# A fused attention and feed-forward kernel: first batch with tokens on partitions, its opening in the planner, new positions

## The chip, the cores and the metric

The kernel runs on one core of one Trainium2 chip. The metric is the device time of one execution in microseconds. A core has five engines with queues of their own: TensorE (PE, matrix products; its weight loads are PEld), VectorE (DVE), ScalarE (ACT), GpSimd (POOL) and SyncE (SP). PE writes into eight PSUM banks of 128 x 512 float32; all other data on the chip lies in SBUF.

## The reference

For each of 8 batches and 8 heads, with 1024 tokens of 64 values, the keys and values are first projected along the tokens to 64 rows, then plain softmax attention runs against those rows, and its output (8192 tokens of 512 values) goes through a gated feed-forward layer.

```python
k_proj = np.einsum('ks,bhsd->bhkd', E, k)
v_proj = np.einsum('ks,bhsd->bhkd', F, v)
scores = scale * np.matmul(q, k_proj.transpose(0, 1, 3, 2))
scores = scores - np.max(scores, axis=-1, keepdims=True)
attn = np.exp(scores)
attn = attn / (np.sum(attn, axis=-1, keepdims=True) + 1e-09)
attn_out = np.matmul(attn, v_proj)          # then (B, H, S, D) -> (B * S, H * D)
gate = 1.0 / (1.0 + np.exp(-(x @ w_gate)))  # x: 8192 x 512, w_gate, w_val: 512 x 1536
out = gate * (x @ w_val) @ w_out            # w_out: 1536 x 512
```

## The kernel before

**Units of work.** Tokens are handled in 16 blocks of 512, two to a batch. A block needs its part of the attention output, transposed (tiles `xT`), then the gate and value products (`wG`, `wV`), the gating into `hT`, and the output product with `wO`. Matmul operands are bfloat16. Blocks 1 to 15 compute gate and value with seven products in place of eight on halved matrices (`seven`, line 1253, called by `quad_jobs`, 1292): sums of the weights (`w_sum`, 1198, into `tG`, `tV`) and of `xT` (`x_sums`, 1193, into `xS`) are made once, and partial results are added by ScalarE and VectorE. Three such steps K make a block, so block b has K = 3b to 3b + 2, and K counts to 48. The output product does the same (`o_jobs`, 1435; sums `o_sum` of `wO` into `wT`, `s_sum` of `hT`), except in block 0 and in the last block, where it is plain (`o_plain`, 1411). Block 0's gate and value products are plain too (`plain_steps`, 1135): 96 matmuls of 512 columns.

**The attention of batches 1 to 7.** `kv` projects k and v of a batch in one bank (1560); ScalarE keeps the result in `kpd` and `vpD`, and SP transposes `kpd` to `kpD` and q to `qT` by DMA (`turn_kd`, `transpose_q`). A score tile holds 128 tokens on the partitions and 4 heads times 2 groups of 64 rows (`score`, 1699). VectorE takes the maxima of its eight groups (`highest`); they are subtracted either by TensorE with a matmul of 512 columns against `minus`, or by VectorE (`lower`, 1731; the choice is `s0` to `s7`, one for each of a batch's eight tiles). ScalarE takes the exponential into `pt`, SP transposes by DMA to `eT`, and `outs` multiplies with `vpD`, whose extra column of ones gives the sums. VectorE takes their reciprocal and divides by them, or ScalarE copies the bank out and GpSimd divides (`d0` to `d2`, one for each of three groups of heads), into `xt`, which SP transposes into `xT`. `pt` and `xt` lie in the buffer `KVs` that the loads of k and v fill. In batch 1, k and v are projected one after the other (`apart_jobs`), and q and `kpd` are transposed by TensorE (`turn_q_pe`, `turn_kd_pe`).

**The first batch.** It has another form: scores lie with the projected rows on the partitions, the exponential is taken without a maximum, the sums come from a matmul with a pattern (`h_den`), a reciprocal of 128 columns (`h_rec`) and a second matmul that spreads them (`h_bc`), and VectorE multiplies the output with them (`h_scale`). The first 512 tokens (block 0) run in an order written out by hand (lines 1010 to 1063), with matmuls on `ident` as fillers (`busy`); the second 512 (block 1) are jobs (`second_half`, 1078).

**What sets the order.** From 21.8 us on, every piece of work is a job with an engine, a position, a release time and a cost by a model (`Scheduler`, 148). The planner steps through modelled time and gives each free engine the ready job of lowest position, as long as its position is within `window` of the first unplaced PE job, and PSUM banks and buffers can be had. The outcome is a fixed order for each queue. Positions come from the table `AT`. POOL first issues all loads of `start_loads` (624) in order: these DMAs convert float32 to bfloat16.

Of the kernel before, what the change touches and what calls it, by code (L numbers as in the profile page):

```python
# [7 lines left out]
ALU = mybir.AluOpType  # L8
# [16 lines left out]
    window=2.535, step=0.142, lag=0.29, ostep=0.443, tanh=1.746, hidden=-1.635, oa=0.798, ob=3.658,  # L25
    sums=1.354, late=0.034, sc=1.515, scs=0.326, out=4.0, outs=0.181, loads=1.714, gap=0.063,
    kv=5.561, tq=3.75, xa=6.242, xb=6.53, w0=3.112, ws=0.6, kv1=2.867, vv1=3.987, wo=3.716, f_wo=0,
    qt1=2.06, sc1=4.73, scs1=0.041, late1=0.543, out1=4.796, outs1=0.123, osum=4.574, loads2=7.657,
    tq2=5.48, kv2=7.388, xa2=5.884, xb2=1.618, o0=4.191, o0s=0.26, xs1=4.106, sc2=1.232, end=4.616,
    pesub=0.843, s0=1, s1=1, s2=1, s3=0, s4=0, s5=0, s6=0, s7=0, o0p=1, o1p=0, o2p=0, o3p=1, x1=0,  # L30
    x2=0, x3=0, x4=0, g1=0, g2=0, g3=0, g4=1, d0=1, d1=0, d2=0, dsub=-0.833, dexp=0.747, dinv=0.205,
    ddiv=1.082, dplus=0.007, dsnap=-1.085, dmerge=-0.547, dcopy=0.897, dturn=-0.257, pdma=0.454,
    pact=0.007, pdve=0, ppool=0.112, lag0=0.208, lag1=-0.622, lag2=0.103, lag3=0.091, lag4=0.09,
    lag5=0.002,
# [113 lines left out]
class Scheduler:  # L148
# [4 lines left out]
    def __init__(self, banks, bufs, t0, window, landed):  # L153
        self.jobs, self.now, self.t0, self.window, self.landed = [], None, t0, window, landed
        self.writers, self.readers = {}, {}
        self.free = {
            "bank": {b: t0 for b in banks},
            "buf": {b: t0 for b in bufs},
        }
        self.clean = {b: False for b in banks}  # L160
        self.groups = []
        self.reads = []
        self.more = {"ACT": AT["pact"], "DVE": AT["pdve"], "POOL": AT["ppool"]}

    def job(self, eng, pos, body, release=0.0, name=""):
        j = Job(eng, pos, body, release, name)
        self.jobs.append(j)
        self.now = j
        body()
        self.now = None  # L170
        return j
# [72 lines left out]
    def take(self, j, t):  # L244
        got = []
        for s in j.slots:
# [4 lines left out]
            if s.kind == "bank":  # L251
                if s.clean:
                    mine = [b for b in mine if self.clean[b]]
                elif s.dirty:
                    rough = sum(not c for c in self.clean.values()) + sum(self.clean[b] for _, b in got)
                    mine = [b for b in mine if not self.clean[b] or rough < 3]
# [54 lines left out]
    def run(self):  # L311
        engines = ("PE", "ACT", "DVE", "POOL", "SP")
        self.busy = {e: self.t0 for e in engines}
# [15 lines left out]
        while left:  # L329
            moved = True  # L330
            while moved:
# [4 lines left out]
                for e in engines:  # L336
# [9 lines left out]
                    if best is not None:  # L346
                        self.open[e].remove(best)
                        self.place(best[3], t)
                        left -= 1
                        moved = True  # L350
# [9 lines left out]
def bass_linformer_attn__then__ffn_glu_sigmoid_kernel(  # L360
# [20 lines left out]
    with contextlib.ExitStack() as es:  # L381
# [28 lines left out]
        pats = within([P, 4, 32], FP32)  # L410
        identf = within([P, P], FP32)
        bsel8f = within([P, 4, 2, 64], FP32)
        early[0], used[0] = wT[:, :, :, :].rearrange("p a b c -> p (a b c)"), 0
        bsel8 = within([P, 4, 2, 64], BF16)
        kp = within([P, NR, DH], BF16)
        rhi = within([P, 256], BF16)
        rhl = within([P, 256], BF16)
        kpD0 = within([P, H, DH], BF16)
        vpD0 = within([P, H, DH], BF16)
        rden = within([P, 256], FP32)  # L420
        quad = sbuf("quad", [P, 1], FP32)
        row_f = sbuf("row_f", [P, 1], FP32)
        rows = sbuf("rows", [P, 4, 32], FP32)
        half = sbuf("half", [P, 2], FP32)
        ident = sbuf("ident", [P, P], BF16)
        dsel8 = sbuf("dsel8", [P, 2, 4, 32], BF16)
# [23 lines left out]
        xu = ost  # L450
# [10 lines left out]
        F0, F1, F2, F3, A0, A1, A2, A3 = range(8)  # L461

        plan = Plan()
        sched = Scheduler(range(8), range(2 + NB), 21.8, AT["window"], 38.8)
# [6 lines left out]

        class Ring:
            def __init__(self, banks):
                self.banks, self.turn = banks, 0

            def next(self):
                b = self.banks[self.turn % len(self.banks)]
                self.turn += 1
                return b

        whole = Ring(
            (A0, A1, A2, A3, F0)
            + (A0, A1, F1, F2, A2)
            + (A3, F0, A0, A1, F1)
            + (A3, F0, A2)
            + (F2, A0, A1, F1)
            + (A3, A2, A0, A1, A3, A0)
        )
# [67 lines left out]
        def total(eng, o, a, b, op, r, w, n):  # L556
            fn = lambda e: e.tensor_tensor(o, a, b, op)  # L557
            if eng == "POOL":
                pool(fn, r, w, cost=n / 410 + 0.06, port=True)
# [8 lines left out]
        def load(o, i, w, sem, r=(), nbytes=0):  # L568
            add("POOL", lambda e: e.dma_start(o, i), r=r, w=w, dma=sem, cost=0.88, nbytes=nbytes)  # L569
# [14 lines left out]
        def load_kv_heads(n, src, R):  # L584
            hh = slice(4 * R, 4 * R + 4)
            load(
                KV[n][:, hh, :],
                src[0].rearrange("h (p t) d -> p h (t d)", t=NT)[:, hh, :],
                [("KV", n, R)],
                f"KV{n}{R}",  # L590
            )
# [32 lines left out]
        def start_loads():  # L624
# [24 lines left out]
            load_w(3)  # L649
            load_w(4)  # L650
            load_w(5)

        def constants():
# [10 lines left out]
            dve(lambda e: e.tensor_copy(pats[:, 0, :], count[:, 0:32]), ["count"], ["pats"])  # L664
            for i, n in ((1, 8), (2, 4)):
                dve(
                    lambda e, i=i, n=n: e.tensor_copy(
                        pats[:, i, :].rearrange("p (a b) -> p a b", b=n),
                        count[:, 0:n].unsqueeze(1).to_broadcast([P, 32 // n, n]),
                    ),  # L670
                    ["count"],
                    ["pats"],
                )
            dve(
                lambda e: e.tensor_scalar(
                    pats[:, 3, :].rearrange("p (a b) -> p a b", b=16),
                    count[:, 0:16].unsqueeze(1).to_broadcast([P, 2, 16]),
                    8.0,
                    -1.0,
                    op0=ALU.is_ge,  # L680
                    op1=ALU.mult,
                ),
                ["count"],
                ["pats"],
            )
            dve(
                lambda e: e.transpose(
                    rows[:, :, :].rearrange("p a b -> p (a b)"),
                    pats[:, :, :].rearrange("p a b -> p (a b)"),
                ),  # L690
                ["pats"],
                ["rows"],
            )
            dve(
                lambda e: e.tensor_tensor(row_f[:, :], rows[:, 0, 0:1], quad[:, :], ALU.add),
# [11 lines left out]
            if any(AT[f"s{n}"] > 0 for n in range(8)):  # L707
                dve(
                    lambda e: e.tensor_scalar(
                        minus[:, :], count[:, :], row_f[:, 0:1], -1.0, op0=ALU.is_equal, op1=ALU.mult  # L710
                    ),
                    ["count", "row_f"],
                    ["minus"],
                )
            for n, op in ((0, ALU.is_ge), (1, ALU.is_lt)):
                dve(
                    lambda e, n=n, op=op: e.tensor_scalar(
                        half[:, n : n + 1], row_f[:, :], 64.0, None, op0=op
                    ),
                    ["row_f"],  # L720
                    [("half", n)],
                )
            for t, k, m, w in ((dsel8, "dsel8", 8, 4),):
                for n in range(2):
                    for i in range(w):
                        dve(
                            lambda e, t=t, m=m, n=n, i=i: e.tensor_scalar(
                                t[:, n, i, :].rearrange("p (a b) -> p a b", b=m),
                                count[:, 0:m].unsqueeze(1).to_broadcast([P, 32 // m, m]),
                                half[:, n : n + 1],  # L730
                                2.0 * i,
                                op0=ALU.subtract,
                                op1=ALU.is_equal,
                            ),
                            ["count", ("half", n)],
                            [(k, n)],
                        )
            for t, k, m, i, v in (
                (bsel8f, "bsel8f", 8, 1, 0.25),
                (bsel8, "bsel8", 8, 1, 0.5),  # L740
            ):
                dve(
                    lambda e, t=t, m=m, i=i, v=v: e.tensor_scalar(
                        t[:, :, :, :].rearrange("p c h d -> p (c h) d"),
                        count[:, 0:m].unsqueeze(2).to_broadcast([P, m, 64]),
                        rows[:, i, 0:1],
                        v,
# [1235 lines left out]
```

## Time and profile before

| | us |
|---|---|
| median of three runs (lowest, highest) | 529.25 (528.47, 529.41) |
| the profiled execution | 528.34 |
| its span, first to last instruction | 526.5 |
| busy: PE, DVE, ACT, POOL | 512.5, 434.3, 372.2, 127.3 |

The granted TensorE clock was 0.999 in the mean. A line of a group gives the kernel's line, engine, operation, tiles and shapes, the count, then the busy time and the mean length of one instruction in ns, then the idle time of the engine just before them and what ended it. Matmuls and VectorE instructions overlap their neighbours, so the mean length is more than the distance from start to start. Line 528 is the helper of all matmuls, 542 of all ScalarE instructions and 569 of all loads. Times in the text are us from the span's start.

### The profile page before, as it was taken

Reading aid. Unit: us, or ns where it says so; the run is one execution under the profiler, and the core shown is the slowest. Engines: PE = TensorE matmul, PEld = TensorE weight load, DVE = VectorE, ACT = ScalarE, POOL = GpSimd, SP = SyncE. Lnnn points to the kernel's source line nnn. Section 1 sums busy time; section 2 is a strip of 40 time slices with the busy share of each in tenths; the row PEclk is TensorE's granted clock in tenths of the full one; section 3 lists DMA queues with packets and bytes.
Section 4 is the critical chain, followed back from the end, with each engine's and each line's share of the span. In section 5 each row is a group of like instructions: output and inputs, shape, how many; then the busy total and the mean of one; then the engine's idle time right before and its main releaser. Section 6 shows DMA issues by size and latency. Waiting matters only on the chain.

```text
span 526.5 us, 12200 instructions
## 1 busy us (share of the span) xinstructions
PE 512.5 (97%) x4823; PEld 427.1 (81%) x4826; DVE 434.3 (82%) x862; ACT 372.2 (71%) x689; POOL 127.3 (24%) x146
## 2 busy tenths in 40 slices
PE   4999989999999999999999999999999999999997
PEld 4545847878988898888988899878988889888883
DVE  6579798879997899779996899968997799978570
ACT  2556965867786878768878687768777688766661
POOL 9710002602232044020530214220440205011200
PEclk9999999999999999999999999999999999999999
DMA  9999738995699657974689565994369956210103
GB/s 159 199 198 205 123 73 168 160 182 121 101 168 212 95 134 131 230 137 114 104 130 225 99 152 82 189 193 94 107 121 231 152 105 107 71 41 21 62 30 131
DMA packets 134569, 70.53 MB, mean 134 GB/s; under 512 B 92912, under 2 KB 126192, under 8 KB 134512
## 3 DMA queue, kind: packets, MB, share of 16 engines
q0 software_dynamic: 34320, 29.89, 36.6%
q1 hardware_dynamic: 100192, 39.86, 36.6%
q8 instruction: 38, 0.62, 0.5%
q14 instruction: 19, 0.16, 0.1%
HBM read 60.29 MB, written 16.78 MB: 146 GB/s over the span
## 4 chain that ended last, share of the span: by engine, by line
PE 86%; DMA 9%; POOL 1%; ACT 1%; DVE 1%; issue 1%; POOLq 0%; SPq 0%; ACTq 0%
PE pA L528 45%; PE pF L528 41%; DMA KVs<-in_v_dram 8%; DMA xT<-KVs 1%; POOL KVs L569 1%; ACT spare L542 1%; ACT KVs L542 0%; POOL Qb L569 0%; DVE spare L1247 0%; DVE wT L917 0%; DVE KVs L1807 0%; DVE hT L1316 0%; DVE wT L823 0%; ACT ost L542 0%; ACT vpD L542 0%
## 5 line engine op out<-in xcount | busy, mean ns | idle before, releaser
L542 ACT ACTIVATE spare<-pF 128x512 f32<-128x512 f32 (+1 forms) x165 | 95.2, 589 | 41.7 <-PE pF L528 39.6
L557 POOL TENSOR_TENSOR hT<-hT,hS 128x512 bf16<-128x512 bf16 x42 | 52.4, 1272 | 263.0 <-PE pA L528 122.2
L542 ACT ACTIVATE spare<-pA 128x512 f32<-128x512 f32 (+1 forms) x117 | 67.9, 586 | 32.0 <-PE pA L528 30.5
L528 PE MATMUL pA<-wO,hT 128*128 128x256 bf16 (+1 forms) x370 | 54.4, 286 | 1.0 <-ACT spare L542 1.0
L542 ACT ACTIVATE spare<-spare 128x512 f32<-128x512 f32 x71 | 44.5, 628 | 11.4 <-DVE spare L1247 11.2
L1247 DVE TENSOR_TENSOR spare<-pF,spare 128x512 f32<-128x512 f32 x57 | 39.1, 687 | 12.4 <-ACT spare L542 11.1
L1316 DVE SCALAR_TENSOR_TENSOR hT<-spare,pF 128x512 bf16<-128x512 f32 x59 | 40.1, 682 | 11.1 <-PE pF L528 7.4
L1247 DVE TENSOR_TENSOR spare<-pA,spare 128x512 f32<-128x512 f32 x53 | 36.0, 686 | 13.0 <-ACT spare L542 5.9
L528 PEld LDWEIGHTS pA<-wO,hT 128*128 128x128 bf16 x372 | 36.1, 98 | 9.8 <-DVE topf L1720 1.0
L1316 DVE SCALAR_TENSOR_TENSOR hT<-spare,pA 128x512 bf16<-128x512 f32 x54 | 36.7, 682 | 6.0 <-PE pA L528 5.6
L528 PE MATMUL pF<-xT,wG 128*128 128x256 bf16 (+1 forms) x244 | 39.3, 283 | 0.4 <-ACT pF L542 0.4
L528 PE MATMUL pF<-xS,tG 128*128 128x256 bf16 x256 | 38.4, 273 | 0.0
L528 PE MATMUL pF<-wO,hT 128*128 128x256 bf16 (+1 forms) x227 | 35.3, 295 | 0.1
L528 PE MATMUL pA<-wT,hT 128*128 128x256 bf16 x264 | 35.0, 273 | 0.2 <-ACT spare L542 0.2
L528 PE MATMUL pA<-xT,wV 128*128 128x256 bf16 (+1 forms) x208 | 33.9, 285 | 0.0
L528 PE MATMUL pF<-xT,wV 128*128 128x256 bf16 (+1 forms) x200 | 32.8, 286 | 0.0
L528 PE MATMUL pA<-wT,hS 128*128 128x256 bf16 x240 | 31.4, 272 | 0.0
L528 PE MATMUL pF<-xS,wV 128*128 128x256 bf16 x208 | 31.2, 273 | 0.0
L528 PEld LDWEIGHTS pF<-xT,wG 128*128 128x128 bf16 x244 | 23.6, 98 | 6.4 <-ACT pF L542 0.7
L528 PE MATMUL pA<-xS,wG 128*128 128x256 bf16 x192 | 28.6, 273 | 0.0
L528 PEld LDWEIGHTS pA<-wT,hT 128*128 128x128 bf16 x264 | 25.4, 98 | 3.2 <-ACT spare L542 0.5
L528 PEld LDWEIGHTS pF<-wO,hT 128*128 128x128 bf16 x228 | 22.1, 98 | 7.2
(193 smaller groups left out, 1252.2 us busy)
## 6 DMA issues: line engine op xcount, KB each, us to landing
out_dram<-ost SPq DMA_DIRECT2D x64, 256.0 KB, 2.8
KVs<-in_k_dram POOLq DMA_DIRECT2D x16, 512.0 KB, 7.7
KVs<-in_v_dram POOLq DMA_DIRECT2D x16, 512.0 KB, 13.4
Qb<-in_q_dram POOLq DMA_DIRECT2D x14, 512.0 KB, 17.9
wO<-in_moe_w_out_dram POOLq DMA_DIRECT2D x1, 1536.0 KB, 12.8
wG<-in_moe_w_gate_dram POOLq DMA_DIRECT2D x5, 256.0 KB, 19.2
wV<-in_moe_w_val_dram POOLq DMA_DIRECT2D x5, 256.0 KB, 19.9
Qb<-in_q_dram POOLq DMA_DIRECT2D x4, 256.0 KB, 14.7
```

What stands on the lines that cost most here:

```text
L528: lambda e: e.matmul(o, lhsT, rhs, **kw),
L542: lambda e: e.activation(o, i, func, scale=scale),
L557: fn = lambda e: e.tensor_tensor(o, a, b, op)
L569: add("POOL", lambda e: e.dma_start(o, i), r=r, w=w, dma=sem, cost=0.88, nbytes=nbytes)
L1247: lambda e: e.tensor_tensor(PB(b)[:, :] if stay else BF(s), PB(b)[:, :], BF(s), ALU.add),
L1316: lambda e: e.scalar_tensor_tensor(o, y.rearrange("p (j c) -> p j c", j=2), 1.0, x.rearrange("p (j c) -> p j c", j=2), ALU.add, ALU.mult,),
```

## The change

- The first batch takes the form of the others: tokens on partitions, maximum and subtraction, exponential into a buffer. The sum (`total0`) and its reciprocal follow on VectorE, and the weights are multiplied with it before the product with v (`norm0`, on GpSimd for heads 0 to 3 of the first 512 tokens, else on VectorE). TensorE transposes them (`turn_p0`), and four products in quarters of the array give the output already transposed (`h_xo`), which is copied into `xT`. `h_den`, `h_rec`, `h_bc`, `h_scale` and their patterns go.
- All of it is jobs of the planner, which starts at 8.3 us in place of 21.8; fillers are put where PE has nothing before 21.0 modelled us.
- Loads of the first k, and of half the first v, are halved (25 issues in place of 22); weights come in the order 0, 3, 1, 4, 2, 5; block 0's products follow that order.
- The memsets of `kpd` and `vpD` move from GpSimd to VectorE and to the start.
- Batch 1 projects k and v together and turns q and k by DMA. The load of `wO` no longer waits for v.
- `s0` to `s2` become 0, `d2` becomes 1; four weight sums go to GpSimd; keys of dependences are finer (a half of the heads each).
- Costs in the model change, all positions are new, `window` goes from 2.535 to 39.691.
- The last quarter of the last block is computed, copied and stored in two halves of 256 columns.

```diff
 AT = dict(
-    window=2.535, step=0.142, lag=0.29, ostep=0.443, tanh=1.746, hidden=-1.635, oa=0.798, ob=3.658,
+    window=39.691, step=0.195, lag=0.031, ostep=0.461, tanh=24.746, hidden=-7.261, oa=0.642, ob=4.537,
...
-    pesub=0.843, s0=1, s1=1, s2=1, s3=0, s4=0, s5=0, s6=0, s7=0, o0p=1, o1p=0, o2p=0, o3p=1, x1=0,
-    x2=0, x3=0, x4=0, g1=0, g2=0, g3=0, g4=1, d0=1, d1=0, d2=0, dsub=-0.833, dexp=0.747, dinv=0.205,
+    xa2=2.02, xb2=5.69, o0=8.301, o0s=1.088, xs1=-1.514, sc2=-4.038, end=3.656, pesub=8.049, s0=0, s1=0, s2=0,
+    s3=0, s4=0, s5=0, s6=0, s7=0, o0p=1, o1p=0, o2p=0, o3p=1, x1=0, x2=0, x3=0, x4=0, g1=0, g2=0, g3=0, g4=1,
+    d0=1, d1=0, d2=1, dsub=-4.028, dexp=-11.886, dinv=-7.839, ddiv=-2.87, dplus=-7.33, dsnap=7.354,
...
+FB = dict(
...
+    f_pv00=1, f_pv01=0, f_pv10=0, f_pv11=0, f_s00=0, f_s01=1, f_s10=0, f_s11=1, f_n00=1, f_n01=0, f_n10=0,
...
+    f_dk=1, f_w2=1, f_late=0, f_q1=0, f_q2=0, f_wsG0=0, f_wsG1=1, f_wsG2=0, f_wsV0=0, f_wsV1=0, f_wsV2=0,
...
-        sched = Scheduler(range(8), range(2 + NB), 21.8, AT["window"], 38.8)
+        busy0 = {"PE": 8.3, "ACT": 8.4, "DVE": 7.0, "POOL": 18.3, "SP": 8.3}
+        sched = Scheduler(range(8), range(2 + NB), 8.3, AT["window"], 38.0, busy0, 21.0)
...
             for R in range(2):
-                load_kv_heads(0, k, R)
-            for R in range(2):
+                for th in range(2):
+                    load_part(0, k, R, th)
                 load_q_half(0, 0, R)
-            for R in range(2):
-                load_kv_heads(1, v, R)
+            load_part(1, v, 0)
+            for th in range(2):
+                load_part(1, v, 1, th)
             load_w(0, 0)
             load_w(0, 1)
+            load_w(3)
             load_w(1)
-            load_w(2)
             for R in range(2):
                 load_q_half(0, 1, R)
-            load_w(3)
             load_w(4)
+            load_w(2)
             load_w(5)
...
+        def total0(t, R, s):
+            i = inv[:, 16 * t + 8 * R : 16 * t + 8 * R + 8]
+            x = BF(s).rearrange("p (n k) -> p n k", n=8)
+            ks = [("inv", t, 4 * R + h) for h in range(4)]
+            dve(lambda e: e.tensor_reduce(i, x, mybir.AxisListType.X, ALU.add), [bf_(s)], ks)
+            dve(lambda e: e.reciprocal(i, i), ks, ks, n=30)
+
+        def norm0(t, R, s, eng):
+            i = inv[:, 16 * t + 8 * R : 16 * t + 8 * R + 8].unsqueeze(2).to_broadcast([P, 8, 64])
+            x = BF(s).rearrange("p (n k) -> p n k", n=8)
+            o = pt0[:, t % 2, 512 * R : 512 * R + 512].rearrange("p (n k) -> p n k", n=8)
+            fn = lambda e: e.tensor_tensor(o, x, i, ALU.mult)
...
+            def tile(hf, R, t):
+                new_group()
+                bk = new_bank()
+                sb = None if hf and FB["f_late"] else new_buf()
+                p = FB[f"sc{hf}{R}"] + 0.003 * (t % 2)
+                job("PE", p, lambda: score(t, R, bk), name="sc")
+                job("DVE", p, lambda: highest(0, t, R, bk), name="top")
+                job("PE" if by_pe(0, t, R) else "DVE", p, lambda: lower(0, t, R, bk), name="sub")
...
+                job("ACT", p, lambda: exp0(bk, sb), name="exp")
+                job("DVE", p + FB["dsum"], lambda: total0(t, R, sb), name="psum")
+                eng = "POOL" if FB[f"f_n{hf}{R}"] > 0 else "DVE"
+                job(eng, p + FB["dnorm"], lambda: norm0(t, R, sb, eng), name="norm")
...
-                r=[("pt", 3, 1)] if AT["f_wo"] else [("KV", 1, R) for R in range(2)],
+                r=[] if FB["f_w2"] else [("pt", 3, 1)] if AT["f_wo"] else [("KV", 1, R) for R in range(2)],
...
-        for K in range(3, 6):
-            quad_jobs(K, K)
-        apart_jobs(1, 0, AT["kv1"])
-        apart_jobs(1, 1, AT["vv1"])
-        turn_q_pe(AT["qt1"])
+        for K in range(1, 6):
+            if K > 2 or FB[f"f_q{K}"]:
+                quad_jobs(K, K)
+        if FB["f_dk"]:
+            kv_jobs(1, AT["kv1"])
...
+        if FB["f_dq"]:
+            turn_q(AT["qt1"])
...
             h = hT[blk % 2]
-            for tt in range(4):
+            last = blk == 2 * B - 1
+            for tt in range(3 if last else 4):
...
+            for x in range(2 * last):
+                new_group()
+                b = new_bank()
+                cc = slice(256 * x, 256 * x + 256)
```

More of the change, by code (lines that the diff above doesn't have):

```diff
@@ L312, in run @@
         engines = ("PE", "ACT", "DVE", "POOL", "SP")
-        self.busy = {e: self.t0 for e in engines}
+        self.busy = dict(self.busy0)
         self.pipe, self.held, self.lock = self.landed, 0.0, 0.0
@@ L706, in constants @@
                 )
[L707 to L722, printed above, removed]
@@ L757, in project_consts @@
             for g in range(2):
-                b = whole.next()
+                b = g
                 for t in range(4):
@@ L847, in VPD @@
-        def VPD(R):
-            return [("vpD0", h, g, R) for h in range(2) for g in range(2)]
+                mm(7, bank[7][:, 0:P], ident[:, :], ident[:, :], ["ident"], n=P)
         def h_qt(hf, R, rr, bk):
@@ new lines, in keep_v0, with turns @@
+        def keep_v0(R, bk, g, eng):
+            gg, hh = slice(64 * g, 64 * g + 64), slice(4 * R, 4 * R + 4)
+            i = PB(bk)[gg, 0:256].rearrange("p (h d) -> p h d", h=4)
+            copy(eng, vpD[0][gg, hh, g, 0:DH], i, [], [("vpD", 0, g, R)], bk, 270 if eng == "ACT" else 380)
+        def turns(b, src, keys, n=4):
+            ob = PB(b)[:, :].bitcast(BF16)
+            for x in range(n):
+                mm(b, ob[:, x * P : (x + 1) * P], src(x), ident[:, :], keys + ["ident"], tr=True, n=P)
@@ new lines, in total0 @@
+        def total0(t, R, s):
[9 more added lines that the diff above has]
+            fn = lambda e: e.tensor_tensor(o, x, i, ALU.mult)
+            r, w = [("inv", t, 4 * R + h) for h in range(4)] + [bf_(s)], [("pt0", t % 2, R)]
+            if eng == "POOL":
+                pool(fn, r, w, cost=1.11, port=True)
+            else:
+                dve(fn, r, w)
@@ L1135, in plain_steps @@
         def plain_steps():
-            for m in range(NF):
+            for m in [m for q_ in range(3) for m in (2 * q_, 2 * q_ + 1, 2 * q_ + 6, 2 * q_ + 7) if not (q_ and FB[f"f_q{q_}"])]:
                 new_group()
@@ L1582, in keep_kd @@
                 [],
-                [("kpd", g)],
+                [("kpd", g, x) for x in range(2)],
                 b=bk,
@@ L1685, in turn_kd_pe @@
                     ident[:, :],
-                    [("kpd", 0), ("kpd", 1), "ident"],
+                    [("kpd", g, x) for g in range(2) for x in range(2)] + ["ident"],
                     tr=True,
@@ L1792, in invert @@
                 [],
-                [("inv", t, hh[0])],
+                [("inv", t, h) for h in range(*hh)],
                 b=bk,
```

815 lines of the change are left out of this document (357 added, 458 removed).

## The prediction

> **What bounds the kernel now.** I read the page's busy table, then the waits of TensorE, then busy time by stretches, then the groups of the engines.
>
> ```profile
> span 526.5 us, 12200 instructions
> ...
> PE 512.5 (97%) x4823; PEld 427.1 (81%) x4826; DVE 434.3 (82%) x862; ACT 372.2 (71%) x689; POOL 127.3 (24%) x146
> ```
>
> TensorE is busy for 97% of the span. Its waits (engine, line, released by: sum, times, longest):
>
> ```profile
> PE pA L528 <- DMA EF<-in_F_dram: 5.7, 1, 5.7
> PE pA L528 <- ACT spare L542: 1.9, 3, 1.0
> ```
>
> The first is the start; the second, with two short ones, is 2.3 us of stall between 64 and 73 us. The same by stretches (busy us and instructions of PE, PEld, DVE, ACT, POOL, then granted clock, DMA share, GB/s):
>
> ```profile
> 0.00:20.00 20.00, 12.71 (x181) 9.93 (x181) 11.83 (x36) 7.16 (x15) 19.21 (x33) 1.00 1.08 174
> 20.00:24.00 4.00, 3.58 (x54) 2.15 (x47) 2.62 (x7) 2.65 (x6) 3.40 (x5) 1.00 1.45 195
> 24.00:34.00 10.00, 10.00 (x60) 4.85 (x58) 5.75 (x16) 4.28 (x8) 0.74 (x1) 1.00 1.45 197
> 34.00:50.00 16.00, 16.00 (x143) 7.54 (x142) 15.94 (x39) 9.83 (x20) 0.98 (x2) 1.00 1.29 204
> 50.00:60.00 10.00, 9.99 (x112) 8.45 (x112) 6.35 (x12) 9.32 (x18) 0.78 (x1) 1.00 1.21 198
> 60.00:80.00 20.00, 17.71 (x150) 11.85 (x148) 18.91 (x33) 14.30 (x27) 0.69 (x1) 1.00 0.32 67
> 80.00:510.00 430.00, 429.21 (x4071) 375.30 (x4071) 369.02 (x719) 321.04 (x594) 101.51 (x106) 1.00 0.70 129
> ```
>
> From 80 to 510 us TensorE misses 0.8 us: there every microsecond of matmul counts, and VectorE has room (369 of 430). From 34 to 50 and from 60 to 80 VectorE is full: there its work may count too. So the sum is TensorE's work taken away, against later starts and new stalls.
>
> **Rates.** Busy time of pipelined groups overlaps, so I take distances between starts. The last plain blocks start 12 matmuls of 512 columns every 2.59 us: 0.216 each. Eight 128-column transposes of q last 0.62 with 0.22 for the last one: 0.057 each. VectorE's full-width operations start every 0.60 us, whatever they are:
>
> ```profile
> 72.75 0.69 DVE L1747 TENSOR_TENSOR pF<-pF,topf 128x512 f32<-128x512 f32 x1
> 73.35 0.68 DVE L1720 TENSOR_REDUCE topf<-pA 128x8 f32<-128x512 f32 x1
> 73.95 0.68 DVE L1720 TENSOR_REDUCE topf<-pF 128x8 f32<-128x512 f32 x1
> ```
>
> **1. Subtractions leave TensorE (s0 to s2 become 0).** The groups that go, and those of step 2:
>
> ```profile
> L528 PE MATMUL pF<-top,minus 128*128 128x512 bf16 x13 | 4.8, 379 | 0.0
> L528 PE MATMUL pA<-ident,Qb 128*128 128x128 bf16 x44 | 3.5, 220 | 0.4 <-DMA Qb<-in_q_dram 0.4
> L528 PE MATMUL pA<-top,minus 128*128 128x512 bf16 x8 | 3.0, 379 | 0.0
> L528 PE MATMUL pA<-ident,kpd 128*128 128x128 bf16 x8 | 0.6, 219 | 0.0
> ```
>
> 13 + 8 = 21 matmuls of 0.216: **-4.5 us**, three in each of batches 1 to 7. VectorE takes 21 x 0.60 = 12.6 us more and gives back 28 divisions of 256 columns (d2 becomes 1). A 128x256 division shows 406 ns, about 0.33 between starts: 9.3 us. Net +0.5 us in a batch of 61 us, of which 369/430, or 86%, were busy: covered. ScalarE copies 28 times 260 columns for it (a 256-column copy shows 384 ns; +10 us in all, on 71%), GpSimd divides them (822 ns for 384 columns, so 0.55: +15 us, on 24%). If the cover fails in a batch, TensorE waits; that is rival 2.
>
> **2. Batch 1 turns q and k by DMA.** 32 + 8 transposes x 0.057 = **-2.3 us** of TensorE; VectorE loses 2 evictions and ScalarE 3. The joint projection of k and v is worth under 0.1 (12.2 us in 6 batches against 2.1 for each of batch 1's two parts, busy). In their place come 5 DMA transposes on SP; such an issue takes 1.24 us there and lands after 3.2 to 3.6. Batch 1's scores so come some 4 us later than after a transpose on TensorE, and block 0's stores stand behind these issues on SP. Batch 1 is wanted when block 2 begins, near 81 us, and until then TensorE has blocks 0 and 1: covered unless the loads are late.
>
> **3. First batch, second half of the tokens.** It removes 16 transposes, 16 score, 16 output and 32 sum and broadcast matmuls, 3.5 to 4 us by their rates; it brings 16 + 16 transposes, 16 score matmuls of 128 columns (48 x 0.057 = 2.7), 2 subtractions (0.4) and 16 output matmuls (0.9): 4.0. **0** on TensorE, +-0.5. On VectorE: four maxima 2.4, two subtractions 1.2, four sums with reciprocals 2.8, four products 2.4, about 7 copies or parts 2.6, so 11.4 against 5.6 before (reciprocal 0.95, scalings 3.2, splitting and copies 1.4): +5.8 us between 30 and 50 us, where it was full. Four weight sums move to GpSimd (-1.5), batch 1 has 3 subtractions more and 4 divisions fewer (+0.5) and no q evictions (-1.3): net +3.5 us up to 80 us.
>
> **4. The opening.** Before, plain products start at 21.9, halt for the output matmuls, and count as started at 22.9 (24.66 less the eight done by then). After, the first half's chain is longer: maximum, subtraction, exponential, sum, product, transpose, copy, output, copy. VectorE's first-half share is 12.6 us (4 maxima, 2 subtractions, 4 sums, 2 products, the rest copies), and q arrives about 11.8: it ends at 24.3 at best. The two R=0 products are GpSimd's (f_n00), and stand behind its load issues: 22 issues took from 1.35 to 17.5, 0.73 each, and 25 will end near 19.7. A product of 512 columns is 1.1 (822 x 512/384), so both are done at 21.8, and transpose, copy, output and copy add 1.7 to 2: first plain product near 23.6, the rest of xT near 25. Counted start 24.0 against 22.9: **+1.1**. Ends: -0.5 (VectorE runs without a gap), +3.5 (each of 10 handovers 0.3 later).
>
> **5. From there to 80 us.** Weights in the order 0, 3, 1, 4, 2, 5 arrive as the plain products use them, and w_out no longer waits for v: its issue waited 15.0 us for that landing. Against it stands step 3's +3.5 on a full VectorE. Before, this stretch lost 2.3; the gain could be all of that, the loss all of 3.5. Nearer is a small loss, since 50 to 60 us left VectorE 3.65 us: **+1.0**.
>
> **6. The positions.** All are new, and the planner's window goes from 2.5 to 39.7. The trace cannot price this. The nearest rows: 0.8 us lost from 80 to 510 us, 2.3 in 60 to 80. I take **+1.0**, ends -0.5 and +8 (over 1 us in each of seven batches).
>
> **7. The end.** The last quarter leaves in two halves: the last copy has 256 columns (384 against 600 ns), the last store half the bytes of one that lands in 2.8. **-0.4**, ends -0.2 and -1.
>
> The GpSimd work of steps 1 and 4 meets a row that speaks against it. VectorE's sums of 1024 columns differ by 44 ns:
>
> ```profile
> L557 DVE TENSOR_TENSOR hS<-hT 128x1024 bf16<-128x1024 bf16 x14 | 10.2, 731 | 3.8 <-PE pF L528 2.4 <-PE pA L528 1.2
> ...
> L557 DVE TENSOR_TENSOR hS<-hS,hT 128x1024 bf16<-128x1024 bf16 x14 | 9.6, 687 | 0.2
> ```
>
> By the rows, GpSimd's neighbourhood costs VectorE at most 44 ns in an operation, some 4 us spread over about 90 sums, off the path; the sum takes nothing for it. The Trainium skill, SBUF — State Buffer, section "SBUF: two separate sides", says that GpSimd and a VectorE instruction with two SBUF inputs hold a shared port pair in turn, and that the loser waits for the whole instruction. By that rule, as an estimate, up to 15 us more of GpSimd divisions could each hold such a sum for up to 0.55 us; the rows show a tenth of that as a mean, and only where VectorE is full would it reach TensorE.
>
> **The sum.** -4.5 - 2.3 + 0 + 1.1 + 1.0 + 1.0 - 0.4 = -4.1. The profiled execution took 528.34 (span 526.5 and 1.8 around it), so 524.2 in its terms; it is 0.9 under the median of 529.25. I put the time between the two scales, at **524.5**.
>
> **Rivals.**
> 1. The ramp is bound by VectorE. The opening costs its +3.5 and the whole +3.5 of step 3 turns into stalls before 80 us: 524.5 + 2.4 + 2.5 = 529.4. For it: 15.94 of 16 us. Against: 3.65 us free from 50 to 60, and less batch 1 work on ScalarE, which was 9.32 of 10 there. It ends near no change. Chance 0.14.
> 2. Slower: with all eight subtractions in VectorE's queue between maximum and exponential, a score bank is held for a queue of 0.60 us operations, and matmuls of the blocks wait for banks. At 1.3 us in each of seven batches it costs 9: 524.5 + 9 - 1 = 532.5. It decides from 0.7 us a batch. For it: VectorE at 86% and 2.3 us lost at its fullest stretch. Against: five of eight were there before at 0.8 us lost in 430. Chance 0.14.
> 3. TensorE's relief is not on the path: the circle of turned output, loads of the next k and v, projection and attention sets the pace. The chain of waits does pass through loads of v (8%). Then -4.5 is lost: 529. Against: TensorE waited for those loads 0.4 us in all. Chance 0.06.
> 4. The clock. If TensorE idles for 3 us while the first half's chain runs, and then 16 plain products start at half clock, they take 3.5 us longer: 528. In the trace the clock is 1.00 in every stretch, though TensorE idled up to 5.7 us before its first matmul, so I give it 0.04. The Trainium skill, TensorE: Matmul & The Clock Gate, Part 1, states that the clock falls to half when TensorE has not been busy of late; no run here shows it yet.
>
> **Chances and range.** The forecast holds 0.62, of which about 0.12 lie below 521 (no loss in the ramp, none from the positions). Its own range, with the middle of the ends of steps 4 to 6, is 520 to 527.5. Rivals 1 and 3, 0.20 together, lie about the old time: I split them 0.03, 0.08 and 0.09 over faster by over 0.2%, within 0.2% (1.06 us of 529.25, about what a measurement of this kernel can tell from no change) and slower by over 0.2%. Faster: 0.62 + 0.04 + 0.03 = 0.69; same 0.08; slower 0.14 + 0.09 = 0.23. For eight times in ten the range reaches from 519.5 to 531.5.
>
> **What would show it.** Step 1: no matmul from top and minus in batches 1 to 7 (two or four remain for the first), 56 subtractions there on VectorE. Step 2: no kpd or Qb transposes on TensorE after 50 us, and 28 DMA transposes into qT. Step 4: the first plain matmul between 23 and 24.5; later than 26 makes the forecast wrong. Steps 3 and 5: PE idle of 2 to 5 us in 24 to 80; over 7 favours rival 1. Step 6: PE idle under 3 us from 80 to 510; over 7 there is rival 2. Rival 4 would show as a clock under 1.00.

## The result and the profile after

The changed kernel takes 525.5 us (525.35 to 525.72) against 529.28: a ratio of 0.9932, 95% interval 0.9915 to 0.9949. On a second chip it was 0.9946 (0.9927 to 0.9965). It was forecast at 524.5. The profiled execution took 525.35, 3.0 less than that of before (528.34); the sum had 4.1.

The page's head of the changed kernel:

```profile
span 523.6 us, 12301 instructions
...
PE 510.3 (97%) x4787; PEld 428.8 (82%) x4792; DVE 457.3 (87%) x867; ACT 371.2 (71%) x711; POOL 147.5 (28%) x180
```

Its stretches, in the columns used before (busy us and instructions of PE, PEld, DVE, ACT, POOL, then the granted clock):

```profile
20.00:24.00 4.00, 1.96 (x22) 0.93 (x18) 2.01 (x4) 1.20 (x3) 3.86 (x5) 1.00 1.45 195
24.00:34.00 10.00, 8.70 (x59) 3.80 (x60) 7.59 (x19) 4.14 (x8) 2.38 (x4) 0.83 1.45 196
34.00:50.00 16.00, 15.01 (x97) 7.74 (x96) 15.08 (x28) 7.93 (x15) 4.89 (x5) 1.00 1.29 205
50.00:60.00 10.00, 9.78 (x84) 6.29 (x82) 10.00 (x22) 5.70 (x11) 1.15 (x1) 1.00 1.22 203
60.00:80.00 20.00, 19.95 (x186) 16.29 (x186) 19.82 (x35) 15.74 (x31) 0.00 (x0) 1.00 0.43 69
80.00:510.00 430.00, 429.59 (x4083) 374.15 (x4085) 389.37 (x726) 328.11 (x631) 115.95 (x134) 1.00 0.70 131
```

Two things are to be seen. From 34 us on TensorE loses less than before (34 to 80: 1.26 us in place of 2.30; 80 to 510: 0.41 in place of 0.79), though VectorE carries 24 us more there. And the opening is much worse than forecast: TensorE is busy for 1.96 us of 20 to 24, and from 24 to 34 its clock is 0.83. Its waits:

```profile
PE pF L528 <- DMA EF<-in_F_dram: 5.5, 1, 5.5
PE pF L528 <- POOL wT L996: 2.0, 2, 1.7
PE pA L528 <- ACT eT L542: 1.0, 1, 1.0
PE pA L528 <- ACT spare L542: 1.0, 1, 1.0
```

L996 is `norm0`, the product on GpSimd. TensorE's queue in the opening, in order of time:

```profile
19.84 0.63 PE L528 MATMUL pF<-KVs,EFT 128*64 128x256 bf16 x8
22.15 0.40 PE L528 MATMUL pF<-ident,wT 128*128 128x128 bf16 x4 [1.68 <-POOL wT L996]
22.38 0.38 PE L528 MATMUL pA<-top,minus 128*128 128x512 bf16 x1
...
27.09 1.01 PE L528 MATMUL pF<-xT,wG 128*128 128x512 bf16 x2
27.90 1.06 PE L528 MATMUL pA<-xT,wV 128*128 128x512 bf16 x2
...
30.50 1.02 PE L528 MATMUL pF<-xT,wG 128*128 128x512 bf16 x4
```

The first plain products start at 27.1, before at 21.9. Two of 512 columns take 0.81 us to the next pair at 27.9, where the rate is 0.43: that is half clock. Eight of them are done when the next four start at 30.50. GpSimd's queue tells why the first product was late:

```profile
18.99 0.93 POOL L569 DMA_DIRECT2D wV<-in_moe_w_val_dram  x1
19.72 1.21 POOL L569 DMA_DIRECT2D wO<-in_moe_w_out_dram  x1
21.06 1.04 POOL L996 TENSOR_TENSOR wT<-EF,inv 128x512 bf16<-128x512 f32 x1
22.05 0.83 POOL L569 DMA_DIRECT2D KVs<-in_v_dram  x1
22.89 1.06 POOL L996 TENSOR_TENSOR wT<-EF,inv 128x512 bf16<-128x512 f32 x1
```

The 25 load issues end at 19.7, as worked out. But the issue of w_out's load follows, and a load of v comes between the two products: they end at 22.10 and 23.95, not both at 21.8. In TensorE's queue the subtractions of the next tiles stand behind the transposes that wait for these products, so the other half of the heads is held as well.

One part of the change is not as it was told. The changed kernel has `f_dk=0`, not `f_dk=1`: batch 1 still projects k and v one after the other, and TensorE still transposes its `kpd`, with eight matmuls at 66.2 us. Of the 16 in this row the first batch has the other eight:

```profile
L528 PE MATMUL pF<-ident,kpd 128*128 128x128 bf16 x16 | 1.4, 219 | 0.0
```

Six DMA transposes make `kpD`, as before. Only q moved to DMA (28 transposes into `qT`, before 24), so 32 transposes left TensorE, not 40.

### The profile page after: what moved, and what is told of

Same layout as the page of the kernel before. It is cut to its first block, busy times and chain, and to the rows that moved or that the text cites. A ratio compares the mean times of both kernels' runs of the same rounds, so it can differ in the third digit from the quotient of the medians.

```text
span 523.6 us, 12301 instructions
## 1 busy us (share of the span) xinstructions
PE 510.3 (97%) x4787; PEld 428.8 (82%) x4792; DVE 457.3 (87%) x867; ACT 371.2 (71%) x711; POOL 147.5 (28%) x180
## 4 chain that ended last, share of the span: by engine, by line
PE 93%; DVE 4%; DMA 1%; ACT 0%; issue 0%; POOL 0%; SPq 0%; DVEq 0%
PE pA L528 47%; PE pF L528 46%; DVE hT L1066 1%; DMA EF<-in_F_dram 1%; DVE wT L996 1%; DVE inv L989 0%; DVE top L1645 0%; ACT spare L542 0%; DVE xT L886 0%; DVE wG L557 0%; DVE topf L1645 0%; POOL wT L996 0%; DVE tV L557 0%; DVE inv L990 0%; DVE pA L1672 0%
## 5 line engine op out<-in xcount | busy, mean ns | idle before, releaser
L542 ACT ACTIVATE spare<-pF 128x512 f32<-128x512 f32 (+2 forms) x164 | 92.4, 581 | 36.4 <-PE pF L528 30.6
L542 ACT ACTIVATE spare<-pA 128x512 f32<-128x512 f32 (+2 forms) x153 | 87.8, 584 | 32.8 <-PE pA L528 23.0
L1734 POOL TENSOR_TENSOR KVs<-spare,inv 128x384 bf16<-128x384 f32 (+1 forms) x51 | 37.0, 731 | 77.8 <-ACT spare L542 66.3
L528 PE MATMUL pA<-wO,hT 128*128 128x256 bf16 (+1 forms) x334 | 45.6, 280 | 0.1
L528 PE MATMUL pF<-wO,hT 128*128 128x256 bf16 (+1 forms) x273 | 41.4, 295 | 0.2
L528 PE MATMUL pF<-xT,wG 128*128 128x256 bf16 (+1 forms) x208 | 34.6, 289 | 0.3 <-DVE xT L886 0.2
L528 PEld LDWEIGHTS pF<-wO,hT 128*128 128x128 bf16 x276 | 26.5, 98 | 8.5
L528 PE MATMUL pA<-xT,wG 128*128 128x256 bf16 (+1 forms) x200 | 32.4, 284 | 0.0
L528 PE MATMUL pF<-xS,tV 128*128 128x256 bf16 x208 | 31.2, 272 | 0.0
L528 PE MATMUL pA<-xS,tG 128*128 128x256 bf16 x184 | 27.6, 273 | 0.0
L528 PE MATMUL pF<-xS,tG 128*128 128x256 bf16 x176 | 26.4, 273 | 0.0
## 6 DMA issues: line engine op xcount, KB each, us to landing
KVs<-in_v_dram POOLq DMA_DIRECT2D x15, 512.0 KB, 10.3
wO<-in_moe_w_out_dram POOLq DMA_DIRECT2D x1, 1536.0 KB, 26.1
```

What stands on the lines that cost most here:

```text
L528: lambda e: e.matmul(o, lhsT, rhs, **kw),
L542: lambda e: e.activation(o, i, func, scale=scale),
L1734: fn = lambda e: e.tensor_tensor(xto.rearrange("p (g h d) -> p h g d", g=2, h=H)[:, hh[0] : hh[1], :, :], o[:, :, 0:DH].rearrange("p (h g) ...
```

## The experiments

Most of these kernels keep the order of work that the planner found, and change what a job does, or where it stands, when it is written out; so the rest of the program is the same. Exceptions are the one planned anew and the two with the last quarter undivided. Where a diff says "order kept", the edit stands between the first line of this and its loop:

```python
order = sched.run()
...
for j in order:
    j.body()
```

The runs of one group share a chip and the runs of the kernel before. The changed kernel was run on two chips, and some kernels below on others; the kernel before has medians of 528.3 to 529.3 us on these chips, so differences between chips are good to some tenths of a us. Where the clock scatters, executions with the same mean clock are compared.

**The changed kernel again.**

> The changed kernel as it is, for comparison on one chip with the others of this series: 0.9932 of the kernel before.

525.67 us (524.34 to 526.83), against 528.63. Its six executions sort by their mean clock: 524.34 at 1.000, 525.56 to 525.76 at 0.997 (four of them), 526.83 at 0.994. A step of 0.003 is one stretch at half clock, 0.003 x 524 x 2 = 3.1 us long, and costs 1.2 us here. The profile of the one at 0.994 shows two such stretches: the clock is 0.50 from 22 to 25 us and from 29 to 31. What a stretch costs depends on where it lies: with the last quarter undivided (below), an execution at 0.993 took 526.3 us, no more than those at 0.997.

**Step 1 undone in the new order.**

```diff
+ AT.update(s0=1, s1=1, s2=1)   # after sched.run(), order kept
```

> The changed kernel with its order of work kept, but the subtractions of the first three score tiles in batches 1 to 7 made by TensorE again (21 matmuls of 512 columns, 21 VectorE subtractions fewer). Theory (TensorE's work counts one for one from 60 to 510 us): 525.5 + 21 x 0.216 = 530.0, and TensorE's busy time rises by about 4.5. Rival (VectorE, now 389 of 430 us busy, is as near to binding, so that its relief of 12.6 us gives the time back): 525 to 527.

530.03 us (528.66 to 531.48), ratio 1.003 (1.0019 to 1.0041). At clock 0.997 it took 529.7 to 530.2, the changed kernel 525.4 to 525.8; at 1.000 it took 528.66 against 524.34. So +4.3 to +4.4, the 21 matmuls one for one. Stretch 60 to 510 of this kernel, then of the changed one:

```profile
60.00:510.00 450.00, 449.51 (x4264) 390.49 (x4262) 395.10 (x735) 343.61 (x660) 116.12 (x134) 1.00 0.69 129
```

```profile
60.00:510.00 450.00, 449.54 (x4268) 390.43 (x4270) 409.19 (x760) 343.85 (x662) 115.95 (x134) 1.00 0.69 129
```

VectorE lost 14 us of work, and TensorE waited neither more nor less: there is no sign of VectorE as the bound, and the relief of TensorE counts in full.

**Step 1 alone in the old order.**

```diff
+ AT.update(s0=0, s1=0, s2=0)   # in the kernel before, order kept
```

> The kernel before with its order of work kept, but all subtractions by VectorE: this part of the change alone. Theory: 529.3 - 4.5 = 524.8, with TensorE's waits as before. Rival (the change needed its new positions and the divisions on GpSimd to carry 12.6 us more of VectorE work; in the old order the scores come later and TensorE waits): 527.5 to 530, with new TensorE waits on VectorE or ScalarE between 60 and 510 us.

541.38 us against 528.34 (the profiled execution took 543.5), ratio 1.0243 (1.0219 to 1.0266). The same edit that is worth -4.4 in the new order costs 13 in the old. The rival had the direction, and was too mild by 11. Its waits and its stretch:

```profile
PE pF L528 <- ACT KVs L542: 4.7, 8, 0.7
PE pA L528 <- ACT spare L542: 1.7, 3, 0.8
PE pA L528 <- ACT KVs L542: 1.6, 4, 0.5
...
PE pA L528 <- DVE ost L1470: 1.3, 1, 1.3
```

```profile
80.00:510.00 430.00, 420.40 (x3936) 360.58 (x3934) 375.94 (x731) 314.01 (x577) 98.78 (x104) 1.00 0.71 130
```

TensorE now waits 12 times for the exponentials (ACT, into KVs), 6.3 us in all. They come late behind VectorE's subtractions: ScalarE waits for these 30 times, 14.4 us in all, before exponentials, where the kernel before shows 2.2. TensorE starts 3936 matmuls in the stretch where it started 4071. It misses 9.6 us there in place of 0.8. VectorE was busy for 376 of 430 us, less than in the changed kernel: it was not full; its work stood at the wrong place in the queues.

**The same, planned anew from the old positions.**

```diff
- pesub=0.843, s0=1, s1=1, s2=1, s3=0,
+ pesub=0.843, s0=0, s1=0, s2=0, s3=0,
```

> The kernel before with all subtractions on VectorE and the whole order planned anew from the old positions. Theory A (an order planned for the new costs is what the old one lacked): 524 to 527. Theory B (the old positions themselves leave TensorE waiting when the scores pass through VectorE's queue, so that the new positions were needed for the 4.5 us): above 535, with TensorE idle for over 10 us between 80 and 510.

575.95 us (574.65 and 577.24) against 529.01. Theory B, and far beyond its bound:

```profile
80.00:510.00 430.00, 402.17 (x3667) 330.90 (x3665) 352.85 (x691) 291.77 (x543) 92.47 (x100) 0.99 0.70 128
```

TensorE misses 28 us of the same 430. A new plan alone does not serve. But its waits are others than in the run before: 0.5 us for exponentials, and 18 for other results of VectorE, sums and gating above all. In the one order where step 1 pays, the positions, the window, the model's costs and the place of a division (d2) are all new; which of them it needs was not tried. Nor was a new plan from the old positions without step 1, so it is not shown how much of the 47 us is due to the subtractions, and how much to planning anew with positions that suit another plan.

**Batch 1's transposes put back as bare work.**

```diff
- job("PE", p, lambda: score(t, y, bk), name="sc")
+ job("PE", p, lambda: (warm(bk, 5 * (b == 1)), score(t, y, bk)), name="sc")   # 5 matmuls on ident
```

> The changed kernel with its order kept and five filler matmuls of 128 columns ahead of each of batch 1's eight score tiles: the 40 transposes that batch 1 no longer has on TensorE come back as bare work. Theory (its work there counts one for one): + 40 x 0.057 = 2.3 us. Rival (between 34 and 80 us VectorE is full, 9.9 to 15.1 of each 10 to 16 us, and TensorE's work lies beside its queue): + 0 to 0.8 us.

527.92 us (526.60 to 530.06), +2.25 against the median of 525.67. At clock 1.000 five executions took 526.6 to 527.3, against one of 524.34 for the changed kernel: +2.3 to +2.9; at 0.997 one is at +2.1. So the 40 matmuls count one for one, within some tenths. But batch 1's score tiles lie later than the expectation says: the fillers start from 78.8 to 90.4 us, six of the eight groups behind 80, where VectorE has room. The rival, which is about 34 to 80 us, is left open. And 32 transposes went, not 40: four fifths of this, 1.7 to 2.3 us, is the price of what left.

**The last quarter undivided.**

```diff
- last = blk == 2 * B - 1
+ last = False
```

> The changed kernel with the last quarter of the last block undivided, as before; all earlier work keeps its order. Theory: + 0.4 us (last copy 0.60 against 0.38, last store of 256 KB against 128 KB). Rival (the second half's 12 weight loads and the extra store eat it): 0 +- 0.1.

526.25 us (526.07 to 526.36) against 525.67. At clock 0.997 it is 526.25 against 525.67: +0.6. With the better opening below (first edit the same):

> The best opening so far with the last quarter of the last block undivided: the test of the last halving without the clock's scatter. Theory: 0.4 us above the same kernel with it halved. Rival: 0 +- 0.1.

522.84 us, ratio 0.9887 (0.9866 to 0.9908) against 0.9883 (0.9861 to 0.9906) for that opening with the quarter halved, on two chips: +0.2, within the intervals. At clock 1.000 it took 522.0 to 522.9 and the halved one 521.7 to 522.0. So the halving is worth 0.2 to 0.6 us; the second comparison does not resolve it.

**The wait filled, nothing else.**

```diff
+ def warm(b, n):
+     for _ in range(n):
+         mm(b, PB(b)[:, 0:P], ident[:, :], ident[:, :], ["ident"], n=P)
...
+ warm(b, ((26, 4), (3, 2))[R][t])   # ahead of four transposes of the first half
+ warm(bks[0], 18)                   # ahead of the first output product
```

> The changed kernel with its order kept, and 53 filler matmuls of 128 columns placed ahead of four transposes and one output product, where TensorE waits between 20.5 and 26.5 us. Theory (the granted clock fell to half from about 26 to 29.5 us because TensorE had idled): the clock stays at 1.00 and the first plain products and output products run at full speed: 1.2 to 1.7 us less, 523.8 to 524.3. Rival (the slow stretch lay under the wait for the second half of the heads, so that it cost nothing): clock at 1.00, time unchanged at 525.3 to 525.7.

524.48 us (524.44 to 525.25), ratio 0.9928 (0.9916 to 0.9940). The clock was 1.000 in all five executions. Stretches of the changed kernel, then with the fillers:

```profile
26.00:28.00 2.00, 1.76 (x11) 0.80 (x10) 2.00 (x6) 0.59 (x1) 0.18 (x1) 0.58 1.45 196
28.00:30.00 2.00, 2.00 (x13) 0.47 (x12) 1.00 (x3) 0.41 (x1) 0.00 (x0) 0.56 1.45 197
```

```profile
26.00:28.00 2.00, 1.75 (x17) 0.90 (x15) 2.00 (x6) 0.60 (x1) 0.24 (x1) 1.00 1.45 196
28.00:30.00 2.00, 1.98 (x16) 0.74 (x16) 2.00 (x7) 0.60 (x1) 0.00 (x0) 1.00 1.45 196
```

The first plain products start at 27.1 to 27.2 in both, but from 28 to 30 sixteen matmuls run in place of thirteen, and after the first eight plain products the next four start at 29.51 in place of 30.50. The time is that of the changed kernel's one execution at clock 1.000 (524.34), 1.2 under its usual one. So the half clock came from the idling and cost 1.2 us.

**The wait taken away: w_out's load issued after the products.**

```diff
+ order.remove(load_of_wO)
+ order.insert(order.index(second_gpsimd_product) + 1, load_of_wO)
```

> The changed kernel with its order kept, but the load of w_out issued by GpSimd after its two products, not before them. Theory (of the wait for GpSimd, the 1.2 us issue of w_out that the planner put in front is the larger part): first product near 19.8, TensorE's waits for it fall from 2.0 to under 0.8 us, first plain product 1 to 1.5 us earlier, and about as much of the time, more if the clock then stays at 1.00. Rival (the sums of VectorE come just before, so the product could not start earlier): no change beyond 0.3 us.

523.40 us (523.39 to 524.46), ratio 0.9899 (0.9880 to 0.9919). The waits for `norm0` fell from 2.0 to 0.4 us, the first plain products started at 26.1, and the clock was 1.000 in five of six executions. Against 0.9946 that is 2.5 us: about one from the earlier start, 1.2 from the clock. A single load issue, moved by three places in GpSimd's queue, holds nearly as much as the whole change brought.

**The wait taken away: the products on VectorE.**

```diff
- if eng == "POOL":
+ if eng == "POOL" and sched.now is not None:   # planned for GpSimd, written out for VectorE
```

> The changed kernel with its order kept, but the two products for heads 0 to 3 of the first 512 tokens made by VectorE, not by GpSimd behind its load issues. Theory (the opening is late because TensorE waits 1.7 us in its queue for the first GpSimd product, and everything behind it with it): that wait is gone, the first plain product starts 1.5 to 2.5 us earlier than 27.1, time 523 to 524. Rival (VectorE's serial work sets the start; two more products there take back what the wait gives): first plain product at 26.5 to 27.5, time 525 to 526.

522.99 us (522.58 to 523.79), ratio 0.9898 (0.9885 to 0.9911). The first plain product starts at 26.5, only 0.6 earlier, but the wait of 1.0 us near 38 us is gone too (34 to 50: 16.00 of 16), and the profiled execution kept its clock at 1.00. At clock 1.000 it took 522.6 and 522.7, 1.7 under the changed kernel. The start is that of the rival, the time that of the theory: what was gained at 38 us neither had named.

**Besides, four copies of the opening on ScalarE.**

```diff
+ eng = "ACT"   # kpD of heads 4 to 7; one of four vpD; one eT; one xT: written out for ScalarE
```

> The run with the first products on VectorE, and besides four of VectorE's copies of the opening (one each of kpD, vpD, eT and xT) moved to ScalarE, the order kept. Theory (after the GpSimd wait is gone, VectorE, busy without a gap from 15.4 to 29.7 us, sets the start): it loses 1.5 us of work ahead of the second half of the heads, first plain product near 26.0, and 0.5 to 1.2 us less than with the products alone. Rival (the landing of v and the chain's handovers set it): unchanged within 0.3 us.

521.99 us (521.66 to 523.67), ratio 0.9883 (0.9861 to 0.9906): the best of all, 3.7 under the changed kernel on its chip and 6.6 under the kernel before. First plain product at 25.9, and 0.5 to 1.0 us less at clock 1.000 than with the products alone (521.7 to 522.0 against 522.6 and 522.7). That is as the theory said.

**And the first two subtractions on TensorE.**

```diff
+ FB.update(f_s00=1)   # with the edits above, order kept
```

> The best opening so far, and the two subtractions for heads 0 to 3 of the first 512 tokens by TensorE (idle there) in place of VectorE. Theory (VectorE's chain without a gap from 14.7 to 25.5 us sets when the second half of the heads is ready): it loses 1.2 us there, the product matmuls for the second half and the plain products after them start 0.7 to 1.2 us earlier, time 520.8 to 521.4. Rival (landing of v and the copies behind it set it): 521.7 to 522.2.

524.79 us (523.99 to 525.28), ratio 0.9919 (0.9898 to 0.9941): 2 to 3 us worse. The theory fell. TensorE's queue and VectorE's show where:

```profile
17.04 1.61 PE L528 MATMUL pA<-ident 128*128 128x128 bf16 x26
18.58 1.06 PE L528 MATMUL pF<-KVs,EFT 128*64 128x256 bf16 x16
19.58 0.28 PE L528 MATMUL pA<-ident 128*128 128x128 bf16 x2
19.70 0.39 PE L528 MATMUL pA<-kpD,qT 128*128 128x128 bf16 x4
```

```profile
19.04 0.64 DVE L999 TENSOR_TENSOR wT<-EF,inv 128x512 bf16<-128x512 f32 x1
20.13 0.69 DVE L1649 TENSOR_REDUCE top<-pA 128x8 bf16<-128x512 f32 x1 [0.45 <-PE pA L528]
```

VectorE had time now (0.45 us idle), and waited: the scores of the second half of the heads stand behind the projection of v in TensorE's queue. It is not the landing of v that holds this, as the rival has it: the part of v that these 16 matmuls wait for landed at 16.2 us (issued at 6.0, 10.3 until landing). Before them stand 26 fillers, which the planner put in where its model had nothing for TensorE. A run with fewer fillers was not made, so what they cost is open. With and without the edit the maximum comes at 20.1 to 20.2. The rest is a loss: the clock was halved again in two executions of six, and a wait of 1.1 us near 37 came back. Even at clock 1.000 it took 524.0 to 524.9; why that wait returns was not settled.

## Why the prediction was right, and where not

The total held by luck: errors of +4.7 us in the opening and -3.5 elsewhere nearly cancel. By the prediction's own signs the opening was wrong (first plain product at 27.1, and "later than 26 makes the forecast wrong"), and so was step 2 (kpd is transposed on TensorE at 66 us). The others came out: no subtraction on TensorE in batches 1 to 7, TensorE idle for 2.6 us from 24 to 80 and 0.4 from 80 to 510. By its steps, in span (526.5 to 523.6, -2.9):

| Step | forecast | measured |
|---|---|---|
| 1 subtractions | -4.5 | -4.4 (put back in the new order) |
| 2 batch 1's transposes | -2.3 | -1.7 to -2.3 (four fifths of 40 put back) |
| 3 second half | 0 | not measured apart |
| 4 opening | +1.1, ends -0.5 and +3.5 | +5.8, of it 1.2 clock |
| 5 to 80 us | +1.0 | -1.0 |
| 6 positions, 80 to 510 us | +1.0 | -0.4 |
| 7 end | -0.4 | -0.2 to -0.6 |

The measured rows add up to about -2.4; the other 0.5 us is not placed.

*Step 4 failed, beyond its own ends and its mark of 26 us.* By its own count the start is 30.50, by when eight plain products are done, less 1.73: 28.8 against 22.9. It had the products behind GpSimd's load issues, with the right 19.7. It took three things wrongly. It put no other issue between; w_out's was free to go first, since the change takes away its wait for v, and a load of v went between the products. It let the two halves of the heads run side by side, where in TensorE's queue one stands behind the other (and both behind the wait of 1.68 us). And it left the clock to a rival. The step's upper end of +3.5 is also not what ten handovers of 0.3 make of +1.1, and the forecast's range of 520 to 527.5 is not half-way to the ends of steps 4 to 6, which is 521.3 to 530.5.

*Step 2 counted eight transposes too many.* It took those of `kpd` for gone; 32 x 0.057 is 1.8 us, not 2.3. Batch 1's projection and its transposes of `kpd` are as before; only those of q went.

*Rival 4, given 0.04, is what happened*, though not alone. It was priced at 3.5 us for sixteen plain products at half clock; the half clock lasted about 3 us and cost 1.2. On the path throughout, 3.1 us at half speed would cost 1.55; the rest probably lay under other waits. "In the trace the clock is 1.00 in every stretch, though TensorE idled up to 5.7 us before its first matmul" was a poor argument: that idling had fillers behind it, not plain products. The Trainium skill, TensorE: Matmul & The Clock Gate, Part 1, has the clock at full or half, judged over windows of about 3.4 us. The trace agrees: at one-microsecond steps the clock reads 1.00, 0.67, 0.50, 0.50, 0.63, 1.00 from 25 to 31 us, after 6 us of which TensorE was busy for under half.

*Steps 5 and 6 were too gloomy.* The stall of 2.3 us shrank to 1.3 and the 0.8 us to 0.4. VectorE at 91% (389 of 430) did not hold TensorE. That is not because the cover was broad: in the old order, with VectorE less busy, the same subtractions cost 13 us. Rival 2 (a queue of 0.60 us operations holding the score banks, 9 us) describes what happens there, and the new order avoids it. The prediction costed step 1 at full value because VectorE was busy for 86% of a batch, and set against rival 2 that five of eight subtractions were there already. Neither decides: what step 1 is worth depends on step 6, and the two should have been priced as one.

*The GpSimd neighbourhood was undersized.* Sums of the changed kernel on VectorE:

```profile
L557 DVE TENSOR_TENSOR xS<-xT 128x512 bf16<-128x512 bf16 x30 | 20.1, 709 | 0.0
...
L557 DVE TENSOR_TENSOR hT<-hT 128x1024 bf16<-128x1024 bf16 x14 | 15.3, 1092 | 0.0
...
L557 DVE TENSOR_TENSOR hS<-hT 128x512 bf16<-128x512 bf16 x14 | 9.3, 665 | 0.0
```

These had means of 417, 684 and 417 ns before: 30 x 0.29 + 14 x 0.41 + 14 x 0.25 = 18 us of VectorE's time, where the text allowed 4. With step 1's net of 0.5 us a batch this is about the 20 us by which VectorE's busy time grew from 80 to 510 us. The means hide what happens: six of each group are long (1.88, 1.64 and 1.00 us in the mean), once in each of six batches, and the others are as before (0.42, 0.68, 0.41). One batch, VectorE and then GpSimd:

```profile
218.43 1.00 DVE L557 TENSOR_TENSOR hS<-hT 128x512 bf16<-128x512 bf16 x1
219.35 1.64 DVE L557 TENSOR_TENSOR hT<-hT 128x1024 bf16<-128x1024 bf16 x1
...
222.18 1.98 DVE L557 TENSOR_TENSOR xS<-xT 128x512 bf16<-128x512 bf16 x1
```

```profile
217.99 2.45 POOL L557 TENSOR_TENSOR hT<-hT,hS 128x512 bf16<-128x512 bf16 x2 [3.16 <-PE pF L528]
...
222.68 1.20 POOL L557 TENSOR_TENSOR hT<-hT,hS 128x512 bf16<-128x512 bf16 x1
```

Each of the 18 long sums runs beside a GpSimd sum, and none beside one of the new divisions. Two other VectorE sums of 512 columns had begun 0.16 us before a GpSimd sum; these kept their 0.41 us. The kernel before has the same 42 GpSimd sums; they met only four of VectorE's sums there (845 ns in place of 686, which is the 44 ns that I read off the mean). So it is the new order that brought them together, not the work moved to GpSimd. The Trainium skill, SBUF — State Buffer, "SBUF: two separate sides", has the loser wait for the whole instruction. The trace agrees in that each long sum ends 0.3 us (of 1024 columns: 0.55) after the GpSimd sum beside it; but five of the six longest start 0.5 us ahead of that sum, while GpSimd issues a load, and why they wait that early is not shown. It did not reach the time, since TensorE lost only 0.4 us in the stretch.

## What to carry to other kernels

In a program whose queues are fixed by a planner, the price of moving work between engines depends on the order as much as on the rates: the same 21 subtractions gave -4.4 us in the new order, +13 in the old, and +47 with a plan made anew from the old positions. Test such a part with the order kept, in the new order and in the old. In an opening, write down every queue in order, DMA issues and freed loads included, and follow what stands behind each wait; and keep TensorE busy through it, since the idling there was paid a second time at half clock.

## What was not expected of the hardware

- One stretch at half clock after idling in the opening lasted about 3 us and added 1.2 us; executions of one program fell into 524.3, 525.6 and 526.8 us at mean clocks of 1.000, 0.997 and 0.994, which is none, one and two such stretches (profiles show one at 0.997 and two at 0.994). With 53 filler matmuls in the wait all five executions kept 1.000.
- Eighteen VectorE sums of two SBUF operands beside a GpSimd sum took 1.64 us in place of 0.68 (1024 columns), and 1.0 to 2.0 us in place of 0.42 (512 columns). Each ended 0.3 to 0.55 us after the GpSimd sum.
